# Interleaving two batches step by step in a fixed order, in a fused attention and spectral-gate kernel

## The chip, the cores and the metric

One NeuronCore of one Trainium2 chip. The metric is the device time in microseconds (us) of one execution; every kernel here was run several times, the slowest and the fastest of a kernel mostly within 1% of each other. A granted TensorE clock of 1.00 is full speed. PE is TensorE, DVE is VectorE, ACT is ScalarE, POOL is GpSimd. A "period" is the time from one batch to the next in the steady part; there are eight batches, so seven periods and a start and an end.

## The reference, cut to what matters

```python
# q, k, v: (8, 8, 576, 64); p: (8, 8, 32, 64)
p_packed = softmax(p @ k.T / 8) @ v            # 32 packed rows per head
x = softmax(q @ p_packed.T / 8) @ p_packed     # per head, heads then joined: (8, 576, 512)
x1, x2, x3 = split(x @ w_proj)                 # three times 512 columns
x2 = irfft(rfft(x2) * rfft(filter_fft))        # along the 576 positions
out = (x1 * x2 * x3) @ w_out
```

The kernel folds `p_packed` into the projection (`qm`) and does both Fourier transforms as matmuls with constant matrices.

## The kernel before: the parts that the argument touches

A batch goes through six functions. The first ones are the "front", the last ones the "back".

```python
def att1(b):                       # front: K
    for g in range(H // 2):
        tp = pst(...)              # a PSUM bank, one pool of 8
        ... 6 transposes of k into tp
        kT = ...;  copy tp -> kT   # DVE for even g, ACT for odd g
        s1 = pst(...)
        ... 6 matmuls kT x pk -> s1;  ACT: e1 = exp(s1)
    ... pv, z1 = e1 x v, e1 x ones          # 2 x 12 matmuls
    ... DVE: rz1 = 1/z1; ppn = pv * rz1     # normalise
    ... PE: transpose ppn; DVE: copy into the ring R

def att2(b):                       # front: Q
    ... 16 + 4 transposes of q, evicted by DVE
    for ii in range(3):
        ... scores against R; ACT: e2 = exp; DVE: zs = sum, zr = 1/zs
        nc.gpsimd.tensor_tensor(a2n, e2, zr, mult)
    ... six projections qp, cast to qm by ACT

def att3(b):  ...                  # fp, fpt: a2n x forward transform; a2tp: a2n transposed

def moe1(b):                       # gate products: five spectra, 9 DVE products, 4 POOL sums
    for m in range(2):
        fre = spectrum(m)
        fim = spectrum(2 + m)
        ... tt[0..3] on DVE
        nc.gpsimd.tensor_tensor(out=gm[:, m, :], in0=tt[0][:], in1=tt[1][:], op=ALU.subtract)
        nc.gpsimd.tensor_tensor(out=gm[:, 2 + m, :], in0=tt[2][:], in1=tt[3][:], op=ALU.add)
    ...
def moe2(b):  ...                  # back: 8 groups x1, x3, x2 (2 + 2 + 5 matmuls); x2 reads all of gm
def moe3(b):  ...                  # back: 5 outputs o, scaled by ACT into os_, sent out

for b in range(B):
    if b + 2 < B:
        load(b + 2)
    if b + 1 < B:
        att1(b + 1); att2(b + 1); att3(b + 1)
    moe1(b); moe2(b); moe3(b)
```

A scheduler decides the final order of the instructions of each engine.

The softmax here doesn't subtract the row's maximum and nothing guards it: scores larger than these inputs give would overflow.

## Time and profile before

| | before |
|---|---|
| median (seven runs of the later rounds: 355.9 to 358.4) | 357.2 us |
| period | 40 us |
| PE busy, mean granted clock | 79%, 0.865 |
| time at half clock, 2 x (1 - 0.865) x 355.8 us | 96 us |

The clock takes only the values 1.00 and 0.50 here, so the mean gives the time at half clock as worked out in the last row. The list of waits of PE alone shows what the other 21% are (columns: us in total, times, longest):

```profile
PE s_b L226 <- ACT kT_b L222: 13.0, 16, 0.8
PE ppT_b L250 <- DVE ppn_b L245: 11.9, 8, 1.5
...
PE s_b L226 <- DVE kT_b L220: 8.8, 16, 0.6
PE fp_b L320 <- ACT qm_b L309: 8.5, 8, 1.7
PE x_b L381 <- POOL gm_b L359: 5.0, 8, 0.7
```

All of them are waits of a batch for its own previous step. The fourth of the lines shown needs care: the name after the arrow is the semaphore that came last by the profile, but `fp` starts just when POOL's first `a2n` is through. Leaving out the first load of the program, PE's waits add up to 56 us.

### The profile page before, as it was taken

Reading aid. Unit: us, or ns where it says so; the run is one execution under the profiler, and the core shown is the slowest. Engines: PE = TensorE matmul, PEld = TensorE weight load, DVE = VectorE, ACT = ScalarE, POOL = GpSimd, SP = SyncE. Lnnn points to the kernel's source line nnn. Section 1 sums busy time; section 2 is a strip of 40 time slices with the busy share of each in tenths; the row PEclk is TensorE's granted clock in tenths of the full one; section 3 lists DMA queues with packets and bytes.
Section 4 is the critical chain, followed back from the end, with each engine's and each line's share of the span. In section 5 each row is a group of like instructions: output and inputs, shape, how many; then the busy total and the mean of one; then the engine's idle time right before and its main releaser. Section 6 shows DMA issues by size and latency. Waiting matters only on the chain.

```text
span 355.8 us, 5499 instructions
## 1 busy us (share of the span) xinstructions
PE 281.9 (79%) x2162; PEld 170.7 (48%) x2162; DVE 161.6 (45%) x376; ACT 127.1 (36%) x259; POOL 94.7 (27%) x106
## 2 busy tenths in 40 slices
PE   0596777789868896789777896789778896889995
PEld 0135625536454464546354464546354455546462
DVE  2401721548233851648223851648233941648481
ACT  1324153242516234333516144333516144333333
POOL 7240320344015500433015500433002500133230
PEclk9997675699958998599959998699968997599999
DMA  7999961940369004920378014930300012000303
GB/s 274 216 194 203 201 89 9 144 49 3 133 84 118 0 33 116 157 29 2 133 91 110 1 50 109 143 33 3 133 2 0 0 62 72 2 1 3 134 2 133
DMA packets 35626, 29.08 MB, mean 82 GB/s; under 512 B 7888, under 2 KB 30416, under 8 KB 35600
## 3 DMA queue, kind: packets, MB, share of 16 engines
q0 software_dynamic: 29408, 16.52, 35.2%
q1 hardware_dynamic: 5904, 10.65, 8.7%
q10 hardware_dynamic: 288, 1.56, 1.1%
q8 instruction: 17, 0.28, 0.3%
q14 instruction: 9, 0.07, 0.1%
HBM read 35.80 MB, written 9.44 MB: 127 GB/s over the span
## 4 chain that ended last, share of the span: by engine, by line
PE 61%; DVE 14%; POOL 11%; ACT 6%; issue 3%; DMA 3%; POOLq 0%; DVEq 0%; ACTq 0%
PE x_b L381 11%; PE o_b L396 10%; PE pv_b L235 6%; POOL gm_b L359 6%; PE fp_b L320 5%; PE s_b L226 5%; PE hp L204 4%; PE qTp_b L268 4%; DVE zs_b L291 3%; DMA pnat<-in_p_dram 3%; POOL gm_b L360 3%; PE x_b L378 3%; PE x_b L376 3%; DVE ppn_b L245 3%; ACT kT_b L222 3%
## 5 line engine op out<-in xcount | busy, mean ns | idle before, releaser
L381 PE MATMUL x_b<-ac,gm_b 128*128 128x288 f16 x320 | 51.2, 287 | 6.1 <-POOL gm_b L359 5.0
L383 ACT COPY x1s_b<-x_b 128x288 f32<-128x288 f32 x64 | 25.5, 398 | 80.0 <-PE x_b L376 59.8
L381 PEld LDWEIGHTS <-gm_b 128*128 128x128 f16 x320 | 30.0, 98 | 19.9 <-POOL gm_b L359 10.9
L396 PE MATMUL o_b<-wout,y_b 128*128 128x512 f16 (+1 forms) x160 | 38.2, 381 | 0.3
L295 POOL TENSOR_TENSOR a2n_b<-e_b,zr_b 128x512 f16<-128x512 f16 (+1 forms) x24 | 21.0, 896 | 61.2 <-DVE zr_b L294 61.2
L226 PE MATMUL s_b<-pk,kT_b 128*96 128x64 f16 x192 | 17.1, 232 | 21.9 <-ACT kT_b L222 13.0
L359 POOL TENSOR_TENSOR gm_b<-tt_b,tt_b 128x512 f16<-128x512 f32 x16 | 20.3, 1270 | 50.8 <-DVE tt_b L356 50.8
L220 DVE COPY kT_b<-kTp_b 128x576 f16<-128x576 f16 x16 | 7.3, 458 | 58.0 <-PE kTp_b L217 57.8
L320 PE MATMUL fp_b<-wc,a2n_b 128*128 128x512 f16 (+1 forms) x80 | 24.0, 400 | 11.7 <-ACT qm_b L309 8.5
L290 ACT ACTIVATE e_b<-s_b 128x512 f16<-128x512 f32 (+1 forms) x24 | 10.7, 520 | 60.4 <-PE s_b L284 60.4
L398 ACT ACTIVATE os_b<-o_b 128x512 f32<-128x512 f32 (+1 forms) x40 | 23.8, 596 | 22.1 <-PE o_b L396 22.1
L386 DVE SCALAR_TENSOR_TENSOR y_b<-w_b,x_b 128x288 f16<-128x288 f32 x64 | 26.8, 449 | 7.2 <-PE x_b L381 5.5
L385 DVE TENSOR_TENSOR w_b<-x1s_b,x_b 128x288 f32<-128x288 f32 x64 | 27.4, 448 | 4.5 <-ACT x1s_b L383 3.8
L378 PE MATMUL x_b<-a2t_b,qm_b 128*128 128x288 f16 x128 | 26.1, 286 | 3.9 <-ACT x1s_b L383 3.9
L142 POOL DMA_DIRECT2D kn_b<-in_k_dram x8 | 6.4, 805 | 83.5 <-PE kTp_b L217 81.4
L376 PE MATMUL x_b<-a2t_b,qm_b 128*128 128x288 f16 x128 | 26.1, 286 | 1.0
L336 DVE COPY a2t_b<-a2tp_b 128x576 f16<-128x576 f16 x16 | 7.3, 457 | 42.7 <-PE a2tp_b L335 42.6
L226 PEld LDWEIGHTS <-kT_b 128*96 128x96 f16 x192 | 13.3, 145 | 27.0 <-ACT kT_b L222 15.7
L396 PEld LDWEIGHTS <-y_b 128*128 128x128 f16 (+1 forms) x160 | 14.7, 100 | 21.0 <-DVE y_b L386 4.2
L228 ACT ACTIVATE e_b<-s_b 96x384 f16<-96x384 f32 x32 | 15.6, 486 | 25.5 <-PE s_b L226 25.5
L309 ACT CAST qm_b<-qp_b 128x512 f16<-128x512 f32 x48 | 24.0, 606 | 0.0
L235 PE MATMUL pv_b<-vn_b,e_b 96*128 96x256 f16 x96 | 22.9, 411 | 0.0
(71 smaller groups left out, 428.9 us busy)
## 6 DMA issues: line engine op xcount, KB each, us to landing
out_dram<-os_b SPq DMA_DIRECT2D x32, 256.0 KB, 2.2
kn_b<-in_k_dram POOLq DMA_DIRECT2D x8, 576.0 KB, 6.1
vn_b<-in_v_dram POOLq DMA_DIRECT2D x8, 576.0 KB, 6.3
qn_b<-in_q_dram POOLq DMA_DIRECT2D x8, 512.0 KB, 7.7
wp<-in_moe_w_proj_dram POOLq DMA_DIRECT2D x3, 512.0 KB, 14.8
filt<-in_moe_filter_fft_dram SPq DMA_DIRECT2D x2, 512.0 KB, 8.6
out_dram<-os_b SPq DMA_DIRECT2D x16, 64.0 KB, 1.7
wc<-c_wc ACTq DMA_DIRECT2D x1, 800.0 KB, 4.7
```

Source lines behind the costliest of these rows:

```text
L226: nc.tensor.matmul(s1[:, hh, 2 * ii:2 * ii + 2, :], kT[:, hh, ii, :], pk[:, b, 2 * g + hh, :], start=True, stop=True)
L235: nc.tensor.matmul(pv[:, t, :], e1[:, i, ts(t, P)], vn[:, 4 * t:4 * t + 4, ts(i, D)], start=(i == 0), stop=(i == KI - 1))
L309: nc.scalar.copy(out=qm[:, t, ts(c, DM)], in_=qp[:])
L320: nc.tensor.matmul(fp[:], a2n[0:n, i, ts(t, P)], wc[0:n, i, 0:DM], start=(i == 0), stop=(i == 4))
L359: nc.gpsimd.tensor_tensor(out=gm[:, m, :], in0=tt[0][:], in1=tt[1][:], op=ALU.subtract)
L376: nc.tensor.matmul(x1[:], qm[:, t, ts(m, P)], a2t[:, t, cols], start=(t == 0), stop=(t == 1))
L378: nc.tensor.matmul(x3[:], qm[:, t, ds(2 * DM + m * P, P)], a2t[:, t, cols], start=(t == 0), stop=(t == 1))
L381: nc.tensor.matmul(x2[:], gm[:, j, ts(m, P)], ac[:, j, cols], start=(j == 0), stop=(j == 4))
L383: nc.scalar.copy(out=x1s[:], in_=x1[:])
L385: nc.vector.tensor_tensor(out=w[:], in0=x1s[:], in1=x3[:], op=ALU.mult)
L386: nc.vector.scalar_tensor_tensor(out=y[:, m, cols], in0=w[:], scalar=SC_Y, in1=x2[:], op0=ALU.mult, op1=ALU.mult)
L396: nc.tensor.matmul(o[0:n, :], y[:, m, COL0[i]:COL0[i] + n], wout[:, m, :], start=(m == 0), stop=(m == ND - 1))
```

## The change

Its intent: while one batch's step waits, the other batch's step runs. The front now holds the gate products too; front of batch b+1 and back of b are generators that hand over after each step, and the one that has done the smaller share of its own total goes next (`together` in the diff; the totals are `FRONT` and `BACK`). Three PSUM banks belong to the front, five to the back. Inside the front, K transposes run ahead of their scores and the Q transposes come earlier. A fixed order takes the place of the scheduler.

```diff
+    NA = 3
     def pst(name, shape, dtype=FP32):
-        return ps.tile(shape, dtype, tag="ps", name=name)
+        return ps.tile(shape, dtype, tag="pa", name=name, bufs=NA)
+    def psm(name, shape, dtype=FP32):
+        return ps.tile(shape, dtype, tag="pm", name=name, bufs=8 - NA)
 ...
+        k_turn(0)
+        yield 260
+        k_turn(1)
+        yield 260
+        score1(0)
+        yield 270
+        k_turn(2)
+        yield 260
+        score1(1)
 ...
+        score1(2)
+        yield 270
+        q_turn(0)
+        yield 450
+        score1(3)
+        yield 270
+        q_turn(1)
+        yield 450
 ...
+    def together(*stages):
+        live = [[0.0, total, g] for g, total in stages]
+        while live:
+            x = min(live, key=lambda r: r[0] / r[1])
+            try:
+                x[0] += next(x[2])
+            except StopIteration:
+                live.remove(x)
+
+    ctx.enter_context(tc.manual_schedule())
+    FRONT, BACK = 11500.0, 13200.0
 ...
-        if b + 1 < B:
-            att1(b + 1)
-            att2(b + 1)
-            att3(b + 1)
-        moe1(b)
-        moe2(b)
-        moe3(b)
+        stages = [(back(b), BACK)]
+        if b + 1 < B:
+            stages.append((front(b + 1), FRONT))
+        together(*stages)
```

The weights after `yield` are PE times in ns.

More of the change, by code (lines that the diff above doesn't have):

```diff
@@ L107 @@
     sb = ctx.enter_context(tc.tile_pool(name="sb", bufs=2))
-    ps = ctx.enter_context(tc.tile_pool(name="ps", bufs=8, space=bass.MemoryType.PSUM))
+    ps = ctx.enter_context(tc.tile_pool(name="ps", bufs=3, space=bass.MemoryType.PSUM))
     pro = ctx.enter_context(tc.tile_pool(name="pro", bufs=1))
+    NA = 3
     def pst(name, shape, dtype=FP32):
-        return ps.tile(shape, dtype, tag="ps", name=name)
+        return ps.tile(shape, dtype, tag="pa", name=name, bufs=NA)
+    def psm(name, shape, dtype=FP32):
+        return ps.tile(shape, dtype, tag="pm", name=name, bufs=8 - NA)
     ident = const.tile([P, P], FP16, tag="ident", name="ident")
@@ L208, with front, k_turn @@
     st = {}
-    def att1(b):
+    def front(b):
         kn, vn, qn, qt = loaded[b]
+        s = st[b] = {}
+        R = rings[b % NR]
+        Rd = R.rearrange("p (g a) c -> p g (a c)", a=2)
         e1 = sb.tile([KP, KI, HJ], FP16, tag="e1", name=f"e1_b{b}")
-        for g in range(H // 2):
+        kTs, qT = {}, sb.tile([P, H, 2, P], FP16, tag="qT", name=f"qT_b{b}")
+        qTt = sb.tile([P, H // 2, 64], FP16, tag="qTt", name=f"qTt_b{b}")
+        def k_turn(g):
             tp = pst(f"kTp_b{b}", [P, 2, 3, KP], FP16)
@@ L217, in att1 @@
                     nc.tensor.transpose(tp[:, hh, ii, :], kn[:, 2 * g + hh, ts(ii, P)], ident[0:KP, 0:KP])
-            kT = sb.tile([P, 2, 3, KP], FP16, tag="kT", name=f"kT_b{b}", bufs=4)
+            kT = kTs[g] = sb.tile([P, 2, 3, KP], FP16, tag="kT", name=f"kT_b{b}", bufs=4)
             if g % 2 == 0:
@@ L222, in att1, with score1 @@
                 nc.scalar.copy(out=kT[:], in_=tp[:])
+        def score1(g):
             s1 = pst(f"s1_b{b}", [KP, 2, KI, NPK])
@@ L225, in att1 @@
                 for ii in range(3):
-                    nc.tensor.matmul(s1[:, hh, 2 * ii:2 * ii + 2, :], kT[:, hh, ii, :], pk[:, b, 2 * g + hh, :],
+                    nc.tensor.matmul(s1[:, hh, 2 * ii:2 * ii + 2, :], kTs[g][:, hh, ii, :], pk[:, b, 2 * g + hh, :],
                                      start=True, stop=True)
@@ L230, in att1, with q_turn, q_tail @@
                 in_=s1[:], func=AF.Exp, scale=scale)
+        def q_turn(c):
+            tp = pst(f"qTp_b{b}", [P, 4, 2, P], FP16)
+            for hh in range(4):
+                for ii in range(2):
+                    nc.tensor.transpose(tp[:, hh, ii, :], qn[:, 4 * c + hh, ts(ii, P)], ident[:])
+            nc.vector.tensor_copy(out=qT[:, 4 * c:4 * c + 4, :, :], in_=tp[:])
+        def q_tail():
+            tp = pst(f"qTtp_b{b}", [P, H // 2, 64], FP16)
+            for g in range(H // 2):
+                nc.tensor.transpose(tp[:, g, :], qt[:, 2 * g:2 * g + 2, :], ident[0:64, 0:64])
+            nc.vector.tensor_copy(out=qTt[:], in_=tp[:])
+        k_turn(0)
[8 more added lines that the diff above has]
+        yield 270
+        k_turn(3)
+        yield 260
+        score1(2)
[3 more added lines that the diff above has]
+        score1(3)
+        yield 270
+        q_turn(1)
+        yield 450
         pv = pst(f"pv_b{b}", [P, 2, 4 * D])
@@ L239, in att1 @@
                                  start=(i == 0), stop=(i == KI - 1))
+            if t == 0:
+                yield 810
         rz1 = sb.tile([P, 2], FP32, tag="rz1", name=f"rz1_b{b}")
@@ L246, in att1 @@
                                     in1=rz1[r, :].unsqueeze(2).broadcast_to([32, 2, D]), op=ALU.mult)
+        yield 810
+        q_tail()
+        yield 150
         pT = pst(f"ppT_b{b}", [P, 2, P], FP16)
@@ L250, in att1 @@
                 nc.tensor.transpose(pT[u * D:(u + 1) * D, t, :], ppn[:, t, :], ident[:])
-        R = rings[b % NR]
         for u in range(2):
@@ L254, in att1 @@
                                   in_=pT[u * D:(u + 1) * D].rearrange("p t (h j) -> p (t h) j", j=NPK))
-        st[b] = dict(R=R)
-    def att2(b):
-        kn, vn, qn, qt = loaded.pop(b)
-        s = st[b]
-        R = s["R"]
-        Rd = R.rearrange("p (g a) c -> p g (a c)", a=2)
-        qT = sb.tile([P, H, 2, P], FP16, tag="qT", name=f"qT_b{b}")
-        qTt = sb.tile([P, H // 2, 64], FP16, tag="qTt", name=f"qTt_b{b}")
-        for c in range(2):
-            tp = pst(f"qTp_b{b}", [P, 4, 2, P], FP16)
-            for hh in range(4):
-                for ii in range(2):
-                    nc.tensor.transpose(tp[:, hh, ii, :], qn[:, 4 * c + hh, ts(ii, P)], ident[:])
-            nc.vector.tensor_copy(out=qT[:, 4 * c:4 * c + 4, :, :], in_=tp[:])
-        tp = pst(f"qTtp_b{b}", [P, H // 2, 64], FP16)
-        for g in range(H // 2):
-            nc.tensor.transpose(tp[:, g, :], qt[:, 2 * g:2 * g + 2, :], ident[0:64, 0:64])
-        nc.vector.tensor_copy(out=qTt[:], in_=tp[:])
+        yield 230
         e2 = sb.tile([P, 5, HJ], FP16, tag="e2", name=f"e2_b{b}")
@@ L277, in att2, with score2 @@
         zr = sb.tile([P, 5, H], FP32, tag="zr", name=f"zr_b{b}")
-        for ii in range(3):
+        def score2(ii):
             n = P if ii < 2 else 64
@@ L299, in att2, with project @@
                 op=ALU.mult)
-        s["a2n"] = a2n
-        qm = sb.tile([P, 2, DM3], FP16, tag="qm", name=f"qm_b{b}")
+        qm = s["qm"] = sb.tile([P, 2, DM3], FP16, tag="qm", name=f"qm_b{b}")
+        def project(c, t):
+            qp = pst(f"qp_b{b}", [P, DM])
+            for u in range(2):
+                g = 2 * t + u
+                nc.tensor.matmul(qp[u * D:(u + 1) * D, :], Rd[:, g, NPK:3 * NPK], wp[:, g, ts(c, DM)],
+                                 start=True, stop=True)
+            nc.scalar.copy(out=qm[:, t, ts(c, DM)], in_=qp[:])
+        for ii in range(3):
+            score2(ii)
+            yield 290 if ii < 2 else 140
         for c in (1, 0, 2):
             for t in range(2):
-                qp = pst(f"qp_b{b}", [P, DM])
-                for u in range(2):
-                    g = 2 * t + u
-                    nc.tensor.matmul(qp[u * D:(u + 1) * D, :], Rd[:, g, NPK:3 * NPK], wp[:, g, ts(c, DM)],
-                                     start=True, stop=True)
-                nc.scalar.copy(out=qm[:, t, ts(c, DM)], in_=qp[:])
-        s["qm"] = qm
-    def att3(b):
-        s = st[b]
-        a2n = s["a2n"]
+                project(c, t)
+                yield 230
         fa = sb.tile([P, 2, 640], FP16, tag="fa", name=f"fa_b{b}")
+        a2t = s["a2t"] = sb.tile([P, 2, S], FP16, tag="a2t", name=f"a2t_b{b}")
         for t in range(2):
@@ L321, in att3 @@
             nc.scalar.copy(out=fa[:, t, 0:DM], in_=fp[:])
+            yield 1090
         fp = pst(f"fpt_b{b}", [P, 2, 64])
@@ L329, in att3 @@
                        in_=fp[:].unsqueeze(2).broadcast_to([P, 2, 2, 64]))
-        a2t = sb.tile([P, 2, S], FP16, tag="a2t", name=f"a2t_b{b}")
+        yield 350
         for t in range(2):
@@ L336, in att3 @@
             nc.vector.tensor_copy(out=a2t[:, t, :], in_=tp[:])
-        s["fa"] = fa
-        s["a2t"] = a2t
-    def moe1(b):
-        s = st[b]
-        fa, qm = s["fa"], s["qm"]
-        gm = sb.tile([P, 5, DM], FP16, tag="gm", name=f"gm_b{b}")
+            yield 280
+        gm = s["gm"] = sb.tile([P, 5, DM], FP16, tag="gm", name=f"gm_b{b}")
         def spectrum(m):
@@ L352, in moe1 @@
             fre = spectrum(m)
-            fim = spectrum(2 + m)
             tt = [sb.tile([P, DM], FP32, tag=f"tt{j}", name=f"tt{j}_b{b}", bufs=2) for j in range(4)]
             nc.vector.tensor_tensor(out=tt[0][:], in0=fre[:], in1=hre[:, m, :], op=ALU.mult)
+            nc.vector.tensor_tensor(out=tt[2][:], in0=fre[:], in1=him[:, m, :], op=ALU.mult)
+            yield 430
+            fim = spectrum(2 + m)
             nc.vector.tensor_tensor(out=tt[1][:], in0=fim[:], in1=him[:, m, :], op=ALU.mult)
-            nc.vector.tensor_tensor(out=tt[2][:], in0=fre[:], in1=him[:, m, :], op=ALU.mult)
             nc.vector.tensor_tensor(out=tt[3][:], in0=fim[:], in1=hre[:, m, :], op=ALU.mult)
@@ L360, in moe1, with back @@
             nc.gpsimd.tensor_tensor(out=gm[:, 2 + m, :], in0=tt[2][:], in1=tt[3][:], op=ALU.add)
+            yield 430
         ft = spectrum(4)
         nc.vector.tensor_tensor(out=gm[:, 4, :], in0=ft[:], in1=htail[:], op=ALU.mult)
-        s["gm"] = gm
-    def moe2(b):
-        s = st[b]
+        yield 430
+    def back(b):
+        s = st.pop(b)
         a2t, qm, gm = s["a2t"], s["qm"], s["gm"]
@@ L371, in moe2 @@
                 cols = ds(e * HALF, HALF)
-                x1 = pst(f"x1_b{b}", [P, HALF])
-                x3 = pst(f"x3_b{b}", [P, HALF])
-                x2 = pst(f"x2_b{b}", [P, HALF])
+                x1 = psm(f"x1_b{b}", [P, HALF])
                 for t in range(2):
                     nc.tensor.matmul(x1[:], qm[:, t, ts(m, P)], a2t[:, t, cols], start=(t == 0), stop=(t == 1))
+                x1s = sb.tile([P, HALF], FP32, tag="x1s", name=f"x1s_b{b}", bufs=3)
+                nc.scalar.copy(out=x1s[:], in_=x1[:])
+                yield 245
+                x3 = psm(f"x3_b{b}", [P, HALF])
                 for t in range(2):
@@ L379, in moe2 @@
                                      start=(t == 0), stop=(t == 1))
+                w = sb.tile([P, HALF], FP32, tag="w", name=f"w_b{b}", bufs=3)
+                nc.vector.tensor_tensor(out=w[:], in0=x1s[:], in1=x3[:], op=ALU.mult)
+                yield 245
+                x2 = psm(f"x2_b{b}", [P, HALF])
                 for j in range(5):
                     nc.tensor.matmul(x2[:], gm[:, j, ts(m, P)], ac[:, j, cols], start=(j == 0), stop=(j == 4))
-                x1s = sb.tile([P, HALF], FP32, tag="x1s", name=f"x1s_b{b}", bufs=3)
-                nc.scalar.copy(out=x1s[:], in_=x1[:])
-                w = sb.tile([P, HALF], FP32, tag="w", name=f"w_b{b}", bufs=3)
-                nc.vector.tensor_tensor(out=w[:], in0=x1s[:], in1=x3[:], op=ALU.mult)
                 nc.vector.scalar_tensor_tensor(out=y[:, m, cols], in0=w[:], scalar=SC_Y, in1=x2[:],
                                                op0=ALU.mult, op1=ALU.mult)
-        s["y"] = y
-    def moe3(b):
-        y = st.pop(b)["y"]
+                yield 610
         for i in range(5):
             n = TILE_SZ[i]
-            o = pst(f"o_b{b}", [P, DM])
+            o = psm(f"o_b{b}", [P, DM])
             for m in range(ND):
-                nc.tensor.matmul(o[0:n, :], y[:, m, COL0[i]:COL0[i] + n], wout[:, m, :], start=(m == 0), stop=(m == ND - 1))
+                nc.tensor.matmul(o[0:n, :], y[:, m, COL0[i]:COL0[i] + n], wout[:, m, :],
+                                 start=(m == 0), stop=(m == ND - 1))
             os_ = sb.tile([P, DM], FP32, tag="os", name=f"os_b{b}", bufs=4)
@@ L404, in moe3 @@
                 nc.sync.dma_start(tl[1], os_[32:64, :])
+            yield 870
+    def together(*stages):
[8 more added lines that the diff above has]
+    FRONT, BACK = 11500.0, 13200.0
     pack_p(0, 1, "a")
     prologue_filter()
-    att1(0)
-    pack_p(1, B, "b")
-    att2(0)
-    att3(0)
+    for _ in front(0):
+        pass
     for b in range(B):
@@ L414 @@
             load(b + 2)
+        if b == 0:
+            pack_p(1, B, "b")
+        stages = [(back(b), BACK)]
         if b + 1 < B:
-            att1(b + 1)
-            att2(b + 1)
-            att3(b + 1)
-        moe1(b)
-        moe2(b)
-        moe3(b)
+            stages.append((front(b + 1), FRONT))
+        together(*stages)
 _INS = ['q', 'k', 'v', 'p', 'moe_w_proj', 'moe_filter_fft', 'moe_w_out']
```

## The prediction

> **What bounds the kernel now.** I read the page's busy table first, then the 40 slices, then a table by stretches, the chain of waits, and last the instructions of single engines in order of time.
>
> ```profile
> PE 281.9 (79%) x2162; PEld 170.7 (48%) x2162; DVE 161.6 (45%) x376; ACT 127.1 (36%) x259; POOL 94.7 (27%) x106
> PEclk9997675699958998599959998699968997599999
> PE 61%; DVE 14%; POOL 11%; ACT 6%; issue 3%; DMA 3%; POOLq 0%; DVEq 0%; ACTq 0%
> ```
>
> TensorE leads by far, but its clock dips in every batch, and 39% of the chain that ends last is not TensorE. So the 79% are partly slow and partly modelled tails, not a full engine. One batch's period is 40 us (the tables of stretches between the starts of the inverse transforms: 39.90, 39.50, 40.20). Cut at the clock's steps it reads:
>
> ```profile
> 134.00:140.40 6.40, 3.61 (x54) 2.58 (x53) 0.91 (x2) 3.37 (x8) 0.82 (x1) 1.00 0.33 107
> 140.40:150.60 10.20, 8.71 (x80) 6.43 (x77) 5.46 (x16) 3.09 (x7) 3.24 (x5) 0.50 1.04 138
> 150.60:174.00 23.40, 21.20 (x134) 11.42 (x133) 12.72 (x28) 8.70 (x19) 7.14 (x7) 1.00 0.22 44
> ```
>
> Columns: stretch, length, busy us of PE, PEld, DVE, ACT, POOL, then granted clock. First the K stage runs thin, then 10.2 us pass at half clock, then it is dense at full clock. The thin stage in order of time on PE:
>
> ```profile
> 135.48 0.45 PE L226 MATMUL s_b<-pk,kT_b 128*96 128x64 f16 x6 [0.55 <-DVE kT_b L220]
> 135.77 0.42 PE L217 MATMUL kTp_b<-ident,kn_b 96*128 96x96 f16 x6
> 137.04 0.46 PE L226 MATMUL s_b<-pk,kT_b 128*96 128x64 f16 x6 [0.85 <-ACT kT_b L222]
> ...
> 144.43 0.42 PE L250 MATMUL ppT_b<-ident,ppn_b 128*64 128x128 f16 x4 [1.49 <-DVE ppn_b L245]
> ```
>
> A K transpose takes 0.29 us of pitch, then PE waits for its eviction. Each wait is one step of a single batch's chain, with nothing of another batch put into it. A period therefore is 27 us of PE work (below), about 5 us that the half clock adds (10.2 us at 0.50), and about 8 us of waits. The chain by line has the same story: softmax normalisation by POOL, `ppn`, and the gate products (`gm`) by POOL.
>
> **What the Trainium skill says.** "TensorE: Matmul & The Clock Gate", "Part 1: The HAM clock gate", says that activity in a window of about 3.4 us releases or re-imposes half clock. The trace agrees: the low stretch is 10.2 us, three such windows, and follows 3.4 us in which PE was busy for 1.96. "Perfetto Trace Analysis", "Optimization Strategy", says that stages with different limits may gain from being interleaved; this change does that. The first page[...] says matmuls keep program order and ACT and DVE are strict FIFO. So a blocked matmul holds all later ones, also those of the other batch; in the trace no later matmul passes one that waits. "PSUM — Partial Sum Buffer", "The four PSUM rules", has one matmul output in at most one of eight banks; so front steps now own three banks and back steps five.
>
> **The change part by part.** The arithmetic is the same: the built program has 4326 PE rows in both. No operation is removed. (1) Front (attention to gate product) of batch b+1 is interleaved with back (inverse transform and output) of b, about one step each. (2) Within the front, K transposes run one or two steps ahead of their scores, and the Q transposes fill the gaps. (3) The order is fixed, without a scheduler. (4) Banks 8 shared become 3 and 5.
>
> PE work of a batch at full clock, from starts in the timeline (runs at half clock halved where the moving stream sets the pace). Front: K transposes 4 x 0.26, scores 4 x 0.29, Q transposes 1.82/2, `pv` and sums 2 x (1.25/2 + 0.21), tails and `ppT` 0.4, second scores 0.7, projections 6 x 0.23, `fp` 2.5, `fpt` 0.71, `a2tp` 0.92, spectra 2.17: 13.5. Back: 8 groups x 1.10 and five outputs in 4.7: 13.5. Sum 27.0. (The step weights in the diff sum to 12.36 + 13.15 = 25.5; they allow too little for `fpt` and `a2tp`.) Other engines busy per period, from the 40.2 us stretch: DVE 19.1, ACT 15.0, POOL 11.2. None bounds a 27 us period on average, but each can stop PE locally.
>
> Which waits does the interleaving cover? I walked the built PE order:
> - K eviction, 0.55 to 0.85 each: two or more steps (0.5 us or more) now lie between; covered.
> - `ppn`: wait 1.49 after z. Now x1, x3, x2 (1.1) and the Q tail (0.15) lie between: 0.35 left.
> - ring copy (0.59 for two, plus wakeups, 0.75) against x1, x3 (0.49): 0.3 left.
> - scores to `fp`: the chain exp, sum, reciprocal, POOL product took 4.3 us before first use; 4.4 us of PE steps now lie between: covered. But six casts (0.48 pitch) and three exps with x1s copies on ACT with three banks: 0.35 left.
> - batch end: five spectra need nine DVE products at 0.60 pitch, 5.6 us. With three front banks f4 waits for the fourth product, and the next K transposes for the sixth and eighth. POOL's four gate sums take 4.95 us, cannot start before the third product (about 2.1 us after f0), and end at 7.1. The first x2 needs the last. From f0's end to x2's end: 7.45 us, with PE work f2 .43, o .93, f1, f3, f4 1.29, x1, x3 .49, two K transposes .52, x2 .61 = 4.27. Left: 3.2.
>
> Sum left 4.2. Clock: dense PE keeps 1.00, except that the hole at batch end has about 1.4 us of work in 4.1, as thin as the window that tripped it. It lasts little longer than a window, so I take half of the periods tripping, each losing 1.7 us (a 3.4 us window at half rate): 0.9. Period: 27.0 + 4.2 + 0.9 = 32.1, instead of 40.
>
> Start and end: the filter prologue ends at 27.1 as before. Front of batch 0 has no partner: K and scores to 31.4, `pv` to 34, `ppT` 35.6, second scores 36.6, `fp` at 40.9 (4.3 later) to 44, `fpt` and `a2tp` to 46, f0 to 46.4, first x2's gate at 53.5 (7.1 later); packing of the other p lies in that wait. The end has no partner either: from the last gate sum, eight groups (8.8, less what lies ahead of it) and outputs 4.7, then 3.7 from the last matmul to the end as now (352.1 to 355.8): 17. Span 53.5 + 7 x 32.1 + 17 = 295; the timed run was 1.9 longer than the span (357.7 to 355.8). Predicted: 296 us.
>
> **Rivals.** (a) *PE fully covered*: if the gate hole is absorbed, period 28 to 29, total about 272. For it: the average load of DVE, ACT and POOL is under 70% of 28. Against: the written order puts x2 third in the new round, so it must wait. (b) *Order and banks bite*: DVE and ACT now serve two chains in written order; a w waiting for x1s holds up the eviction that PE needs, with three front banks. Period 34 to 36, total 310 to 325. For it: the 3.8 us of w waiting for x1s now, and 4 x 0.6 of DVE in a burst. Against: evictions stand in the order in which PE produces. (c) *Clock*: if transposes and small matmuls count little as activity (the thin stage's 1.96 of 3.40 was not enough), half clock returns in the mixed stretches, and 27 us of work becomes 30 or more: total 310 or above. Against: the mixed stretch has dense x and o matmuls every other step. (d) *Loads*: the queue order now puts the five loads at the head of a round. They cost POOL 3.6 us of issue (0.81, 0.77, 0.90, 0.58, 0.58) while it has nothing to compute, and are needed a round later; nothing changes.
>
> **Range and chances.** Period 30 to 34.5 gives 281 to 312; start and end add a few us. I take 279 to 316. Even rival (b) at its worst leaves 10% of gain; only a standing conflict of order with banks in each step could eat 8 us per period. Faster by over 2%: 0.96; within: 0.02; slower: 0.02.
>
> **What would show it.** Clock at 1.00 in nearly all slices between 55 and 275, with a dip at some batch ends; PE busy near 85 to 90% there; waits of PE on `kT` gone from the top of the list; a hole of 2 to 4 us per batch at the first x2, ended by POOL's `gm`, or by DVE's products through the banks; period 32. It would be wrong if the half clock stays in the mixed stretches, if waits for ACT or DVE appear at every step (period over 35), or if the hole at batch end is under 1 us (period under 29.5).

## The result, and the profile after

| | before | after |
|---|---|---|
| median, us (four runs each) | 357.85 | 304.16 |
| ratio, 95% interval | | 0.850 (0.843 to 0.856) |
| period, us | 40 | 33.65, or 32.05 |
| PE busy, mean granted clock | 79%, 0.865 | 85%, 0.958 |
| time at half clock, us | 96 | 25 |
| waits of PE, us | 56 | 29 |

Ratios here and below are the mean time of one kernel's fast runs over that of the other's of the same rounds, so not quite the ratio of the medians. Executions over 1.5% slower than the fastest of the same kernel are left out of the means.

The same three lines of the page as shown before (busy, granted clock by slice, chain by engine):

```profile
PE 256.8 (85%) x2162; PEld 151.5 (50%) x2162; DVE 167.0 (55%) x376; ACT 128.4 (42%) x259; POOL 94.5 (31%) x106
PEclk9999779999979999899999997999979997999999
PE 61%; DVE 14%; POOL 10%; DMA 9%; issue 4%; POOLq 0%; ACT 0%; DVEq 0%; ACTq 0%
```

The broad valleys of the clock have become notches of one slice. And PE's waits:

```profile
PE s_b L320 <- DVE ppk L306: 6.6, 8, 0.8
PE x_b L426 <- POOL gm_b L397: 5.6, 7, 0.8
PE x_b L426 <- POOL gm_b L396: 4.1, 7, 2.1
PE kTp_b L230 <- DVE tt_b L395: 3.2, 6, 0.5
PE f_b L384 <- DVE tt_b L395: 2.4, 8, 0.6
```

The waits for `kT`, `ppn` and `fp` have left the top. What stands there now is the ring copy (`ppk`) and, four times, the gate products: the second to fifth line are one place in the program, the end of a round. Here it is in order of time, on PE and then on POOL:

```profile
148.43 0.59 PE L384 MATMUL f_b<-qm_b,fa_b 128*128 128x512 f16 x2 [0.26 <-DVE tt_b L395]
148.86 0.41 PE L413 MATMUL x_b<-a2t_b,qm_b 128*128 128x288 f16 x2
149.62 0.42 PE L230 MATMUL kTp_b<-ident,kn_b 96*128 96x96 f16 x6 [0.36 <-DVE tt_b L391]
149.88 0.41 PE L419 MATMUL x_b<-a2t_b,qm_b 128*128 128x288 f16 x2
150.82 0.42 PE L230 MATMUL kTp_b<-ident,kn_b 96*128 96x96 f16 x6 [0.53 <-DVE tt_b L395]
151.07 0.29 PE L426 MATMUL x_b<-ac,gm_b 128*128 128x288 f16 x1
151.71 0.42 PE L426 MATMUL x_b<-ac,gm_b 128*128 128x288 f16 x2 [0.35 <-POOL gm_b L396]
152.93 0.42 PE L426 MATMUL x_b<-ac,gm_b 128*128 128x288 f16 x2 [0.80 <-POOL gm_b L397]
```

```profile
147.92 1.28 POOL L396 TENSOR_TENSOR gm_b<-tt_b,tt_b 128x512 f16<-128x512 f32 x1 [11.04 <-DVE tt_b L394]
149.16 1.27 POOL L397 TENSOR_TENSOR gm_b<-tt_b,tt_b 128x512 f16<-128x512 f32 x1
150.39 1.26 POOL L396 TENSOR_TENSOR gm_b<-tt_b,tt_b 128x512 f16<-128x512 f32 x1
151.62 1.26 POOL L397 TENSOR_TENSOR gm_b<-tt_b,tt_b 128x512 f16<-128x512 f32 x1
```

The last sum ends at 152.88, and the last two matmuls of the first x2 start at 152.93. In five of seven round ends the clock then halves for 3.4 us. In the table of stretches around one of them (length, busy us of PE, PEld, DVE, ACT, POOL, then the clock, the DMA share and GB/s) the hole is the first line and its price the second:

```profile
181.50:184.90 3.40, 1.62 (x17) 0.87 (x16) 2.65 (x6) 0.90 (x2) 3.40 (x4) 1.00 0.01 4
184.90:188.30 3.40, 3.32 (x31) 2.89 (x32) 1.11 (x3) 1.37 (x3) 3.40 (x6) 0.51 0.56 60
```

A period with such a notch takes 33.65 us and one without 32.05 (from the starts of POOL's first sums: 80.59, 114.25, 147.92, 179.98). So one trip costs 1.6 us.

Why five and not seven? In the clock records of each of the fourteen traces, all changes lie whole multiples of 3.41 us apart (here the trips start at 85.98, 120.12, 184.97, 219.10 and 253.24, which is 10, 19, 10 and 10 times 3.41). So the hole has to be held against this grid. In the grid stretch that ends at each of the five trips PE is busy for 1.81, 1.82, 1.62, 1.74 and 1.90 us of 3.41. In the two round ends that kept the clock, a grid boundary cuts the hole in two; for the one of the timeline above it is at 150.83:

```profile
147.42:150.83 3.41, 2.26 (x17) 1.07 (x16) 3.41 (x7) 0.85 (x2) 2.91 (x3) 1.00 0.20 52
150.83:154.25 3.42, 2.27 (x32) 1.68 (x32) 2.06 (x5) 1.23 (x3) 3.42 (x4) 1.00 0.00 0
```

The other one has 1.87 and 1.83 in its halves (280.54 to 287.36). So the place of the hole on the grid decides as well as its size. Where two executions of this kernel differ, the clock differs too: the fastest of the four runs (301.34 us) had a mean clock of 0.969 instead of 0.958.

A rough balance: PE waits 27 us less, and 71 us less at half clock are worth up to 35 us, together 62; the gain is 54. Not all low-clock time was PE work, and the work itself grew, as shown below.

### The profile page after: what moved, and what is told of

It reads as the page before. It is cut to its first block, busy times and chain, and to the rows that moved or that the text cites. A ratio compares the mean times of both kernels' runs of the same rounds, so it can differ in the third digit from the quotient of the medians.

```text
span 302.5 us, 5508 instructions
## 1 busy us (share of the span) xinstructions
PE 256.8 (85%) x2162; PEld 151.5 (50%) x2162; DVE 167.0 (55%) x376; ACT 128.4 (42%) x259; POOL 94.5 (31%) x106
## 4 chain that ended last, share of the span: by engine, by line
PE 61%; DVE 14%; POOL 10%; DMA 9%; issue 4%; POOLq 0%; ACT 0%; DVEq 0%; ACTq 0%
PE x_b L426 12%; PE o_b L434 10%; PE fp_b L360 7%; POOL gm_b L397 5%; PE qp_b L343 5%; DMA vn_b<-in_v_dram 5%; DMA kn_b<-in_k_dram 5%; POOL gm_b L396 4%; PE x_b L413 4%; PE x_b L419 4%; PE pv_b L284 4%; PE s_b L241 3%; DVE ppn_b L296 2%; PE a2tp_b L376 2%; PE qTp_b L251 2%
## 5 line engine op out<-in xcount | busy, mean ns | idle before, releaser
L426 PE MATMUL x_b<-ac,gm_b 128*128 128x288 f16 x320 | 54.7, 297 | 9.7 <-POOL gm_b L397 5.6
L396 POOL TENSOR_TENSOR gm_b<-tt_b,tt_b 128x512 f16<-128x512 f32 x16 | 20.3, 1268 | 84.2 <-DVE tt_b L394 84.2
L427 DVE SCALAR_TENSOR_TENSOR y_b<-w_b,x_b 128x288 f16<-128x288 f32 x64 | 28.6, 448 | 26.8 <-PE x_b L426 23.6
L434 PE MATMUL o_b<-wout,y_b 128*128 128x512 f16 (+1 forms) x160 | 40.4, 382 | 0.0
L345 ACT CAST qm_b<-qp_b 128x512 f16<-128x512 f32 x48 | 26.6, 598 | 2.4 <-PE qp_b L343 2.4
L419 PE MATMUL x_b<-a2t_b,qm_b 128*128 128x288 f16 x128 | 27.5, 298 | 0.0
L413 PE MATMUL x_b<-a2t_b,qm_b 128*128 128x288 f16 x128 | 27.4, 297 | 0.0
L384 PE MATMUL f_b<-qm_b,fa_b 128*128 128x512 f16 x80 | 21.2, 380 | 3.0 <-DVE tt_b L395 2.4
L230 PE MATMUL kTp_b<-ident,kn_b 96*128 96x96 f16 x192 | 15.3, 224 | 5.9 <-DVE tt_b L395 3.2
L397 POOL TENSOR_TENSOR gm_b<-tt_b,tt_b 128x512 f16<-128x512 f32 x16 | 20.2, 1266 | 0.0
L230 PEld LDWEIGHTS <-kn_b 96*128 96x128 f16 x192 | 12.9, 110 | 10.4 <-issue 8.2
L343 PE MATMUL qp_b<-wp,ppk 128*64 128x512 f16 x96 | 17.8, 421 | 0.0
L326 ACT ACTIVATE e_b<-s_b 128x512 f16<-128x512 f32 (+1 forms) x24 | 11.5, 520 | 14.2 <-PE s_b L320 14.2
```

What stands on the lines that cost most here:

```text
L230: nc.tensor.transpose(tp[:, hh, ii, :], kn[:, 2 * g + hh, ts(ii, P)], ident[0:KP, 0:KP])
L343: nc.tensor.matmul(qp[u * D:(u + 1) * D, :], Rd[:, g, NPK:3 * NPK], wp[:, g, ts(c, DM)], start=True, stop=True)
L345: nc.scalar.copy(out=qm[:, t, ts(c, DM)], in_=qp[:])
L413: nc.tensor.matmul(x1[:], qm[:, t, ts(m, P)], a2t[:, t, cols], start=(t == 0), stop=(t == 1))
L419: nc.tensor.matmul(x3[:], qm[:, t, ds(2 * DM + m * P, P)], a2t[:, t, cols], start=(t == 0), stop=(t == 1))
L426: nc.tensor.matmul(x2[:], gm[:, j, ts(m, P)], ac[:, j, cols], start=(j == 0), stop=(j == 4))
```

## The experiments

Times are medians (for e10 of its two fast runs alone); the kernel before ran in each set of rounds at 357 to 358 us. Half-clock time is worked out of the mean granted clock as above.

| run | order | interleaved | order inside the front | us | ratio to before | half clock, us |
|---|---|---|---|---|---|---|
| before | scheduler | no | old | 357.2 | | 96 |
| after | fixed | yes | new | 304.2 | 0.850 | 25 |
| e1 | fixed | no | new | 336.8 | 0.943 | 69 |
| e5: e1 without its own stall | fixed | no | new | 312.2 | 0.874 | 39 |
| e9 | fixed | no | old | 351.4 | 0.983 | 96 |
| e10 | fixed | yes | K old | 341.7 | 0.955 | 83 |
| e11: before, gate products early | scheduler | no | old | 346.9 | 0.971 | 100 |
| e2 | scheduler | yes | new | 283.1 | 0.792 | 8 |
| e3: 8 shared banks | fixed | yes | new | 306.6 | 0.857 | 32 |
| e4: banks 4 and 4 | fixed | yes | new | 304.5 | 0.855 | 18 |
| e6: front weighted 14200 | fixed | yes | new | 277.8 | 0.778 | 14 |
| e7: matmuls without use | fixed | yes | new | 296.1 | 0.828 | 5 |
| e8: e2 and e6 together | scheduler | yes | new | 271.2 | 0.759 | 5 |
| e12: e8, 64-row blocks adjacent | scheduler | yes | new | 267.1 | 0.747 | 3 |

All twelve gave the right result, also e7, whose added matmuls are overwritten. My theory was the prediction's: interleaving carries the gain, and the hole at the round's end is what it leaves. The first rival: the new order inside the front carries it. Batch 0's front, which has no partner, had taken only 21 us, which with 13.5 us of back would be 34.5 per period without any interleaving.

**e1: no interleaving.**

```diff
-        return ps.tile(shape, dtype, tag="pa", name=name, bufs=NA)
+        return ps.tile(shape, dtype, tag="pa", name=name, bufs=8)      # psm too
 ...
-        stages = [(back(b), BACK)]
-        if b + 1 < B:
-            stages.append((front(b + 1), FRONT))
-        together(*stages)
+        if b + 1 < B:
+            for _ in front(b + 1):
+                pass
+        for _ in back(b):
+            pass
```

> Undoes the interleaving alone: fixed order, run-ahead inside the front and all else stay, but front of b+1 runs whole and then back of b; one pool of eight banks for both, as nothing is split any more. Theory A (the interleaving of two batches carries the gain): the waits for ppn, ring, a2n come back and with them half clock, period 37 to 39 us, 328 to 345 us in all. Rival B (the new order inside the front carries it, as front of batch 0 took only 21 us alone, from 27.0 to 48.5, and 21 + 13.5 = 34.5 a period): 300 to 318 us.

Measured: 336.75 us (336.4 to 338.6). By the number this is theory A. By the trace it is not: an ACT line and the PE line that it led to show a stall that the experiment itself had made.

```profile
169.81 0.59 ACT L437 ACTIVATE os_b<-o_b 64x512 f32<-64x512 f32 x1 [4.19 <-DMA out_dram<-os_b]
```

```profile
170.98 0.69 PE L241 MATMUL s_b<-pk,kT_b 128*96 128x64 f16 x6 [3.39 <-ACT kT_b L235]
```

The five output copies now come back to back, there are four output buffers, and the fifth copy waited for the first one's transfer. The K eviction behind it in ACT's written order started only at 170.31, after that copy, and PE waited for the eviction. The run had taken away interleaving and added a stall. It had to be done again.

**e5: no interleaving, without that stall.** SBUF had no room for a fifth buffer (the changed kernel with five does not build: 18.75 KB a partition left where 20 are needed), so the fifth copy goes into a product buffer that is free by then.

```diff
-            os_ = sb.tile([P, DM], FP32, tag="os", name=f"os_b{b}", bufs=4)
+            os_ = sb.tile([P, DM], FP32, tag="os" if i < 4 else "tt0", name=f"os_b{b}", bufs=4 if i < 4 else 2)
```

> The first of these runs (no interleaving) had a stall of its own: ACT's fifth output copy waited 4.2 us for the first output's transfer (four output buffers) and held up the K eviction behind it, PE idle 3.4 us. Here the fifth copy goes to a buffer of the gate products, which is free then; nothing else changes. Theory A' (that stall was most of what set it apart from the changed kernel, and interleaving is worth little): 300 to 312 us. Rival (the front's own waits and half clock are the cost, interleaving is worth at least 15 us): 318 to 330.

Measured: 312.15 us (311.4 to 314.2), a hair above the theory A' range and well below the rival's. So interleaving as it came is worth 8 us, and 45 of the gain are there without it. Its period is 33.7 us (once 35.8), with 1.3 us for `ppn`, 1.2 for the last `y` and 1.5 for `a2n` exposed, all of which the changed kernel hides; the changed kernel has the hole and its clock trips in their place.

**e9: the old order inside the front, not interleaved.** As e5, with K transposes alternating with scores, and the Q transposes after the ring copy.

```diff
-        k_turn(0)
-        yield 260
-        k_turn(1)
-        yield 260
-        score1(0)
- ...
+        for g in range(4):
+            k_turn(g)
+            yield 260
+            score1(g)
+            yield 270
 ...  (q_turn and q_tail moved behind the ring copies)
```

> No interleaving as in the run with the fifth output buffer (312 us), and inside the front the old order back: each K transpose directly before its scores, Q transposes after the ring copies. Theory A (the new order inside the front made most of the 45 us between the kernel before and that run, by its own waits and by keeping the clock): period 37.5 to 39.5, 338 to 356 us. Rival (the gate products put a whole front ahead of their use, or the fixed order, made it): 312 to 325.

Measured: 351.43 us. The order inside the front alone is worth 39 us (351.4 to 312.2). The clock by slices, of e9 and then of e5, shows most of it:

```profile
PEclk9998596589975999589975999589985999589999
```

```profile
PEclk9999897887998999979999999969997999799999
```

PE's waits fall from 57 to 37 us, but half-clock time from 96 to 39 us. A stage that was thin enough to lose the clock is now dense enough to keep it, and what follows it runs at full speed.

**e10: interleaved, only the K run-ahead undone.** The same edit as e9's for K, nothing else.

> Changed kernel with interleaving and banks, only the run-ahead of the K transposes undone. In its PE order three of four transposes stand directly before their scores, with no step of the other batch between. Theory A (a step must lie between, interleaving alone does not do it): three waits of 0.5 to 0.8 us come back per batch, 316 to 324 us. Rival (the other batch's steps cover the eviction anyway): 302 to 306.

Measured: 340.9 and 342.5 us in the two fast runs, 349.5 in the two slow (mean clock 0.866, against 0.882 and 0.878; the median of all four is 345.97). The fast ones, 341.7, are theory A's direction, but about twice its size. Two PE lines:

```profile
177.83 0.69 PE L230 MATMUL kTp_b<-ident,kn_b 96*128 96x96 f16 x6
179.24 0.69 PE L241 MATMUL s_b<-pk,kT_b 128*96 128x64 f16 x6 [0.73 <-ACT kT_b L235]
```

Between this transpose and its score stands no step of the other batch, because two front steps fall due after each x2 step of the back (weight 610 of 13200, against 260 and 270 of 11500). The wait is as long as in the kernel before. I had counted such waits and not the clock: they lie next to the hole at the round's end, and the low stretch there grows from 3.4 to 6.8 or 10.2 us; half-clock time is 83 us. So interleaving without run-ahead gains 10 us (e9 to e10, with e10 still having the new Q order) and with it 8 (e5 to the changed kernel); run-ahead gains 39 us without interleaving (e9 to e5) and 38 with it (e10 to the changed kernel, K alone). So the two gains are nearly independent of each other.

**e11: the kernel before with the gate products early.** The third thing that the change did: the spectra of b+1 are written before the back of b.

```diff
+    moe1(0)
     for b in range(B):
 ...
             att3(b + 1)
-        moe1(b)
+            moe1(b + 1)
```

> The kernel before with one thing of the change: spectra and gate products of b+1 are written before the back of b, as the change has them, instead of directly before their use; scheduler and eight banks stay. Theory A (worth the waits for the gate sums and x1s there, 0.65 and 0.49 us per batch, and some PE waits that the scheduler had filled): 340 to 352 us. Rival (this alone is a large part of the 45 us): under 335.

Measured: 346.91 us, as expected: 11 us of 357. The gate sums are then never waited for, and all else stays, the half clock too. Put in a row, the runs divide the 54 us about so: gate products early 11 (before to e11), the fixed order without interleaving -5 (e11 to e9, which differ in small things too), new order inside the front 39 (e9 to e5), interleaving 8 (e5 to the changed kernel).

**e2: the scheduler instead of the fixed order.** One line out:

```diff
-    ctx.enter_context(tc.manual_schedule())
```

> Undoes the fixed order alone: same written steps and the 3 and 5 banks, but the scheduler may move instructions between them. Its PE order keeps the alternation, yet at the batch end it puts x1, x3 and first x2 matmuls of two or three groups before the blocked spectrum and K transposes. Theory A (written order itself is worth little, the hole at the batch end is what is left): 2 us a period less, 285 to 298 us. Rival (fixed order is what makes interleaving work, the scheduler breaks it): 310 us or more.

Measured: 283.08 us (282.4 to 283.8). The fixed order costs 21 us in the interleaved kernel. In the scheduled program x1, x3 and the first x2 matmuls of two or three groups stand before the blocked spectrum and K transposes, the period from the second round on is 30.4 us each time, and no half clock is seen in any of the round ends.

**e3 and e4: the bank split.** e3 takes one pool of eight for both, e4 sets `NA = 4`.

> Undoes the split of the banks alone: one pool of eight for front and back, written order kept. Theory A: the split takes the small bank waits at the batch end (f4 0.26, K transposes 0.36 and 0.53 per period) but the first x2 waits for the same POOL sum anyway, so within 1% of 304. Rival (three front banks hold PE up): 5 us or more faster. Rival (a shared ring couples front and back, so the split pays): slower by 5 us or more.

> Four front banks and four back banks. Theory A: the bank waits at f4 and the K transposes shrink, the first x2's wait grows by as much: 301 to 305 us. Rival (front banks are the limit): under 298. Rival (back needs five): over 308.

Measured: 306.57 us (304.6 to 307.9) and 304.52 us (302.4 to 307.7; the last counted as slow, the three fast runs have 302.4 to 305.5). The split is worth nothing that these runs can tell from noise. e4 shows why, in two lines of PE's waits to be held against those of the changed kernel:

```profile
PE x_b L426 <- POOL gm_b L396: 11.5, 8, 2.1
...
PE kTp_b L230 <- DVE tt_b L391: 1.7, 6, 0.3
```

With a fourth bank the K transposes no longer wait long for a bank (0.3 at `tt` L395 in all instead of 3.2). PE just arrives earlier at x2 and waits there, 11.5 instead of 4.1 us.

**e7: work without use in the hole.** 17 matmuls of 0.12 us per batch go into the banks of the first x1, x3 and x2 before the real ones overwrite them.

```diff
                 x1 = psm(f"x1_b{b}", [P, HALF])
+                fill = (3, 4, 10) if m == 0 and e == 0 else (0, 0, 0)
+                for _ in range(fill[0]):
+                    nc.tensor.matmul(x1[:], qm[:, 0, ts(m, P)], a2t[:, 0, cols], start=True, stop=True)
 ...  (fill[1] in front of x3, fill[2] in front of x2)
```

> Changed kernel plus 17 matmuls per batch without use (3, 4 and 10 of 128x288, 0.12 us each, 2.0 us) into the banks of the first x1, x3 and x2, overwritten by the real ones: work added into the hole. Theory A (half clock is tripped by the thin hole, 1.6 us a time): no half clock after 50 us, period 32.0 each, 293 to 298 us although work is added. Rival (the trips have another cause, or the filler delays the gate): 304 us or more.

Measured: 296.1 us (295.2 to 296.5). Eight times 2.0 us of added PE work make the kernel 8 us faster. The page's clock line has no notch after the start any more, and the period from the second round on is 32.06 us every time, to 0.02:

```profile
PEclk9999979999999999999999999999999999999999
```

That settles the trips: they come from the thin hole, and cost 8 us.

**e6 and e8: the front ahead.** A larger total for the front makes it run ahead, so that two output steps of the back stand behind the last spectrum.

```diff
-    FRONT, BACK = 11500.0, 13200.0
+    FRONT, BACK = 14200.0, 13200.0
```

> Changed kernel, only the weight of the front raised from 11500 to 14200, so that two output steps (2 x 0.93 us of PE) of the back stand after the last spectrum. Theory A (the hole at the batch end before the first x2, and the half clock that it trips in 5 of 7 periods, are what is left): period 30 to 30.7, 281 to 288 us, no half clock after 50 us. Rival (the work only moves: the steps taken from elsewhere open waits for ring, products or a2n there): 297 us or more.

> The scheduled version (283 us, period 30.4, PE still waits 0.7 for POOL's sums and about 0.4 for an x1s copy in each batch) with the front's weight at 14200 too. Theory A (its hole is covered from both sides): 275 to 280 us. Rival (the scheduler had already filled the hole, what is left is PE work): 281 to 286.

Measured: 277.77 us (276.5 to 280.2) and 271.15 us (270.7 to 271.4), both better than theory A's range. Against e5, the best kernel here without interleaving (312.2), e6 is 34 us faster, so the hole had hidden most of what interleaving can give (e5 was not tuned in the same way). With one number changed, e6's period falls to 29.1 us: the hole and the trips are gone, and some of the wait for the ring copy with them (6.6 to 4.4 us in all). In e8 the period is 28.5, and the steady part (from the second batch on) shows no wait of PE any more:

```profile
PE 247.5 (92%) x2162; PEld 145.1 (54%) x2162; DVE 164.8 (61%) x376; ACT 125.2 (46%) x259; POOL 94.8 (35%) x106
```

**e12: fewer switches of the array.** With no waits left, 28.5 us is PE's work, and I had summed 27.0. The filter matmuls of the prologue, which run without waits in the kernel before, show a cost that no duration contains. Their starts are 0.22 us apart, but 0.31 where a 64-row block follows or precedes a 128-row one:

```profile
18.98 0.38 PE L204 MATMUL hp<-fh,wc 128*128 128x512 f16 x1
19.20 0.38 PE L204 MATMUL hp<-fl,wc 128*128 128x512 f16 x1
19.51 0.39 PE L204 MATMUL hp<-fh,wc 64*128 64x512 f16 x1
19.73 0.38 PE L204 MATMUL hp<-fl,wc 64*128 64x512 f16 x1
20.04 0.39 PE L204 MATMUL hp<-fh,wc 128*128 128x512 f16 x1
```

`fpt` and `a2tp` make two passes over five blocks of which the last has 64 rows. e12 lets the second pass begin with that block, which saves two switches in each:

```diff
-            for i in range(5):
+            for i in (0, 1, 2, 3, 4) if t == 0 else (4, 0, 1, 2, 3):   # a2tp; fpt alike
```

> The fastest so far (scheduler, front's weight 14200, 271.15 us, PE without waits at a period of 28.5), plus: the second pass of fpt and of a2tp takes its 64-row block first, so that the 64-row blocks of both passes follow each other. Theory A (a switch between 128-row and 64-row matmuls costs about 0.09 us, as 0.31 instead of 0.22 between filter matmuls shows; four fewer per batch): 0.36 us a period, 267.5 to 269.5 us. Rival (no such cost there): 270.5 to 272.

Measured: 267.14 us (266.4 to 268.0 in five runs), period 28.1 instead of 28.5. The ten `a2tp` of one batch, in e8 and then in e12; to the start of what follows it is 0.91 and 0.71 us, and for `fpt` 0.70 and 0.50, so 0.1 us for each of the four switches:

```profile
158.76 0.98 PE L376 MATMUL a2tp_b<-ident,a2n_b 128*128 128x128 f16 x10
```

```profile
155.20 0.88 PE L377 MATMUL a2tp_b<-ident,a2n_b 128*128 128x128 f16 x10
```

This is the fastest kernel, 12% below the changed one and 25% below the kernel before.

## Why the prediction was right, and where it was not

The time (296 us against 304.16) and the range hold. Two slips in the working changed little: its span of 295 and the 1.9 us outside the span add up to 297, not 296, and the 0.29 us of pitch that it reads as a K transpose's is that of the score matmuls (its sum then has 0.26 and 0.29). Where it draws on the Trainium skill's "TensorE: Matmul & The Clock Gate", that matmuls keep program order stands there in "Part 3: Packing small matmuls", "The mechanism", and the strict queues of ACT and DVE in the paragraph on engine queue depths. By its steps:

- *The waits that interleaving covers.* Right for K and `a2n`: they are gone from the list. But the prediction put the covering down to the interleaving, with the new order inside the front as its part (2). The runs say the reverse. Run-ahead alone brings 39 us (e9 to e5), interleaving on top of it 8 (e5 to the changed kernel), interleaving without K run-ahead 10 (e9 to e10, fast runs). The total came out well because both were in the PE order that I walked; which of the two did it, I had not asked. In this part the mechanism was not right: that the total fits is partly luck.
- *Batch end: 3.2 us left.* Right, in place and cause. Between f4's and the last x2's start (148.43 to 152.93) PE has 0.36, 0.53, 0.35 and 0.80 us of gaps besides 0.26 before f4, 2.3 in all; each gap is some 0.16 us longer by starts, as the profile counts the tail of the last matmul as busy. That makes about 3.1.
- *`ppn` 0.35 and ring 0.3 left.* The sum of the two is a little low: `ppn` shows no PE gap in the steady part, the ring one of 0.84. The DVE lines in order of time give the reason: in written order, a `w`, a `y` and the Q tail's copy stand before the ring copies, although the transpose that these read was issued at 162.16.

```profile
162.14 0.45 DVE L422 TENSOR_TENSOR w_b<-x1s_b,x_b 128x288 f32<-128x288 f32 x1
162.69 0.45 DVE L427 SCALAR_TENSOR_TENSOR y_b<-w_b,x_b 128x288 f16<-128x288 f32 x1
163.06 0.28 DVE L258 COPY qTt_b<-qTtp_b 128x256 f16<-128x256 f16 x1
163.27 0.58 DVE L306 COPY ppk<-ppT_b 64x256 f16<-64x256 f16 x2
```

  This is rival (b), real but small: 0.5 us a period.
- *Casts on ACT 0.35.* No such gap is in the changed kernel.
- *PE work 27.0.* Too low. 32.05 less the gaps (3.1 at the end, about 1.0 at the ring) leaves 27.9, and the scheduled kernels without waits need 28.5 and 28.1. Part of what the sum lacked is the switch cost, which e12 measured as 0.43 us for four switches; projections (64 columns) cut apart by steps of the other batch show it too, x2 next to them having 0.72 us of pitch for 0.61 (changed kernel, 166.46 and 164.13). That all of the difference is switches was not shown.
- *Clock 0.9 a period.* Right in kind: e7 shows that the hole trips the clock. I took half of the periods and 1.7 us each; it was five of seven and 1.6, so 1.1. That it would be a share and not all or none was right, and so was the reason, a hole not much longer than a window.
- *Start and end.* Gate of batch 0 at 53.5 (measured 52.3), the last 17 us (from the last sum's end at 285.9 to 302.5: 16.6).
- *Banks* were named as a part of the hole. They are, but e3 and e4 show that taking that part away moves the wait to the next line and not the end. *Loads*: nothing changed, as predicted, in these kernels; e1's transfers made a wait only through too few output buffers.

What stays open: the exact limit. Of the full-clock grid stretches of all fourteen traces after the first 20 us, all 66 with PE busy for less than 1.75 us were followed by half clock, 12 of 23 between 1.75 and 1.90 us, and 14 of 915 above, the highest at 2.16. PE's busy time holds modelled tails, so it is not the exact measure of what the clock answers to.

## What to carry to other kernels

Before two chains are interleaved, put a step of distance between producer and consumer inside each chain: here that alone gave most of the gain (39 us), and interleaving gave 8 to 10 as it came. Interleaving paid more only when the joint between rounds had been mended: 34 us from e5 to e6. In a strict order, look at that joint: one blocked matmul holds both chains, and a single weight that lets the producing chain run ahead was worth 26 us. An experiment that takes a part away can add a wait of its own (e1), so read its trace before its time.

## What the Trainium skill lacked or had wrong

- "TensorE: Matmul & The Clock Gate", "Why this matters for your kernels", asks for no PE-idle gaps over about 3 us. Here no gap in the stretch that tripped the clock was longer than 0.85 us: 3.4 us with PE busy for 1.96 (before) or 1.62 (after) were enough. It is a thin window that does it. The same page's "A second HAM failure mode: psum-queue depth-cycling" does tell of a clock that swings because of frequent small idles, but gives no share; here it lies between 1.75 and 2.16 us of 3.41 by the profile's busy time, as told above.
- The same page, "Part 4: PE-mode transpose", says that full clock does not engage for transposes. Ten `a2tp` transposes took 0.99 us at full clock (changed kernel), 1.48 in a stretch at 0.50 (kernel before, batch 0): among other matmuls they do run faster with the clock. Whether they count less as activity, as the page also says, is not settled: a stretch of K transposes and scores tripped with PE busy for 1.99 us (before, 137.02 to 140.43), two of other matmuls held with 1.87 and 1.83 (after, 280.54 to 287.36).
- "TensorEngine Tiling (Array Packing)", "Key Properties", says that changing the tiling mode drains TensorE, without a price. If going from 128-row to 64-row blocks is such a change, which no trace here tells, its price is 0.31 instead of 0.22 us between 128x512 matmuls, and 0.43 us per batch for four switches (e12).
- "Perfetto Trace Analysis", "Matmul Optimizations", asks to use all eight banks, and no page says how to divide them between two interleaved chains. 3 and 5, 4 and 4 and a shared eight, all of which use all of them, gave 304.2, 304.5 and 306.6 us: no difference that these runs can tell from noise.
- No page says that filling a hole with useless matmuls can pay: 16 us of them took 8 us off (e7).
